# Decode attention with a gated feed-forward: outputs gathered two batches at a time, matmuls with unused results, and weight rows in another order

## The chip, the cores and the metric

The kernel runs on one NeuronCore of a Trainium2 chip, alone. The metric is the device time of one execution in microseconds (us). Each number of a run is the median over several executions; the profile is of one further execution, and its "span" is the time from its first to its last instruction.

## The reference, cut to what matters

The input has 8 rows (batches) of 512 numbers. They are normalised, and the same normalised rows go into an attention step over a cache and into a feed-forward part whose result gates the attention's output.

```python
def _A_ref(x, k_cache, v_cache, wq, wo):     # 32 query heads, 8 kv heads, Dh = 128
    W = min(4096, max(256, Sk // 4))         # Sk = 4096: the last 1024 positions
    q = (x @ wq) ...                         # one query per batch and head
    k, v = last W positions, each kv head shared by 4 query heads
    p = softmax(q k^T * Dh ** -0.5)
    return (p v) @ wo                        # wo: 4096 x 512
def _B_ref(x, w_gate, w_up, w_down):         # F = 1792
    return (gelu(x @ w_gate) * (x @ w_up)) @ w_down

xn = layernorm(x)
s = _A_ref(xn, ...)
g = silu(_B_ref(xn, ...))
return x + s * g
```

All tensors are bf16. The part of the caches that is read has 32 MB, the weights have some 14 MB, and there is one query per batch: a program of loads.

## The kernel before, in words

The order of the instructions of each engine is written out by hand (`manual_schedule`, L74); nothing is moved by a planner.

**Loads.** All large loads are issued by SyncE, in one queue. `load_wide` (L95) fills one of 3 wide buffers with 128 rows of up to 16 KB: the two halves of wq (`load_wq`, L100), w_gate and w_up (`load_up`, L113), w_down (`load_down`, L116) and the first half of wo (`load_wo`, L122). `load_kv` (L103) fills one of 14 ring buffers with 1 MB of a k or v cache; the later pieces of wo take ring buffers too. Of wq, w_gate and w_up, partition p holds the rows 4p to 4p+3 one after the other (L93, L114), so a load takes 128 contiguous rows. The loop of L494 issues the v load of group g and the k load of group g+2; in its last passes it issues w_gate, w_up, w_down (L500 to L502) and then wo in six pieces, of 16, 8, 4, 2, 1 and 1 row blocks (L505 to L510). The wide buffer of wo's first piece is w_gate's, so that load waits until w_gate's matmuls are done. The input x comes by two small loads on ScalarE's queue (L143), 8 rows each.

**Start.** x is normalised by VectorE into `xhat` (L214), turned by 4 TensorE transposes (L225) into `xT`, with the row order of the weights; then q is computed (L379), turned and laid out (L400, L408).

**Attention.** There are 16 groups, a batch and a half of the kv heads each. In pass g of the loop TensorE computes the scores of group g (`score`, L267), ScalarE their exponentials (`soft`, L293), VectorE turns them (`turn_p`, L301), and TensorE turns the k tiles of group g+1 (`turn_k`, L251) and multiplies the probabilities of group g-1 with v (`values`, L312). `gather` (L330) then takes the result of group g-1: one fp32 product with ones for the sums (L333), two with a selection matrix (L337), a reciprocal (L346) and a product on VectorE (L347) into `oT_all`.

**End.** `ffn_up` (L416) runs 16 matmuls for w_gate, regroups the attention output (L354), then 16 for w_up (all L424), and the gelu on ScalarE and VectorE. `ffn_down` (L461) runs 14 matmuls with w_down (L465), copies the result (L475), brings it into 32 rows with fp32 matmuls (L478) and forms the gate `g_sb` (L487 to L491). Last come the 128 matmuls with wo (L544), in the order of wo's pieces, most in pairs on two column groups of the array; two DVE operations after the last of them (L558, L559) and the store of 8 KB (L560).

Of the kernel before, what the change touches and what calls it, by code (L numbers as in the profile page):

```python
# [9 lines left out]
ALU = mybir.AluOpType  # L10
AX = mybir.AxisListType
BF16 = mybir.dt.bfloat16
FP32 = mybir.dt.float32
# [3 lines left out]
def kernel(  # L17
# [13 lines left out]
    nc = tc.nc  # L31

    B, Sq, D = A_x.shape
    Hkv, Sk, Dh = A_k_cache.shape[1], A_k_cache.shape[2], A_k_cache.shape[3]
# [4 lines left out]
    F = B_w_gate.shape[1]  # L39
    NDC = D // 128  # L40
# [4 lines left out]
    P = nc.NUM_PARTITIONS  # L45
# [8 lines left out]
    QW = HN * rep  # L54
# [8 lines left out]
    p_pool = ctx.enter_context(tc.tile_pool(name="p_pool", bufs=2))  # L63
    pT_pool = ctx.enter_context(tc.tile_pool(name="pT_pool", bufs=2))
    small = ctx.enter_context(tc.tile_pool(name="small", bufs=3))
    o_pool = ctx.enter_context(tc.tile_pool(name="o_pool", bufs=1))
    ffn_sb = ctx.enter_context(tc.tile_pool(name="ffn_sb", bufs=1))
    ps_t = ctx.enter_context(tc.tile_pool(name="ps_t", bufs=3, space=bass.MemoryType.PSUM))
    ps_sc = ctx.enter_context(tc.tile_pool(name="ps_sc", bufs=1, space=bass.MemoryType.PSUM))
    ps_a = ctx.enter_context(tc.tile_pool(name="ps_a", bufs=1, space=bass.MemoryType.PSUM))  # L70
# [14 lines left out]
    DQ = D // NQ  # L85
    x_sb = persist.tile([32, D], BF16, name="x_sb")
# [3 lines left out]

    wq_rows = A_wq.rearrange("(p k) n -> p (k n)", k=NDC)  # L93

    def load_wide(rows, c0, c1):  # L95
        t = wide_slot()
        nc.sync.dma_start(out=t[:, 0 : c1 - c0], in_=rows[:, c0:c1])
        return t

    def load_wq(h):  # L100
# [9 lines left out]
        )  # L110
        return t

    def load_up(w):  # L113
        return load_wide(w.rearrange("(p k) n -> p (k n)", k=NDC), 0, NDC * F)  # L114

    def load_down():  # L116
        return load_wide(B_w_down.rearrange("(p j) d -> p (j d)", j=FR), 0, FR * D)
# [25 lines left out]
    for t in range(2):  # L143
        c = slice(t * D // 2, (t + 1) * D // 2)
# [3 lines left out]
    ident = consts.tile([P, P], BF16, name="ident")  # L148
    nc.vector.memset(ident, 0.0)
    nc.gpsimd.affine_select(  # L150
        out=ident,
        in_=ident,
# [8 lines left out]
        out=perm.rearrange("p (h q) -> p h q", q=P // 32),  # L161
        in_=ident.rearrange("p (q h) -> p h q", q=P // 32),
# [3 lines left out]
    ones_f = consts.tile([P, P], FP32, name="ones_f")  # L166
# [5 lines left out]
        out=hot.rearrange("n r (m j) -> n r m j", m=HN),  # L172
# [21 lines left out]
        out=selq,  # L194
# [18 lines left out]
    nc.vector.reciprocal(out=rstd, in_=rstd)  # L213
    xhat = persist.tile([32, D], BF16, name="xhat")  # L214
    nc.vector.tensor_scalar(  # L215
        out=xhat,
        in0=x_sb,
        scalar1=mv[:, 0:1],
        scalar2=rstd[:, 0:1],
        op0=ALU.subtract,  # L220
# [3 lines left out]
    for k in range(NDC):  # L224
        nc.tensor.transpose(  # L225
            xT_ps[:, k, :],
            xhat.rearrange("b (p k) -> b k p", k=NDC)[:, k, :],
            ident[0:32, 0:32],
        )
    xT = persist.tile([P, NDC, 32], BF16, name="xT")  # L230
# [70 lines left out]
    def turn_p(g):  # L301
        p, acc = p_t[g]
        pT = pT_pool.tile([P, 512], BF16, name="pT")
        nc.vector.transpose(out=pT, in_=p)  # L304
        pT_t[g] = pT
        ss = small.tile([P, QW], FP32, name="ss")
        nc.vector.tensor_scalar(
            out=ss, in0=selq, scalar1=acc[:, 0:1], scalar2=None, op0=ALU.mult
        )
        ss_t[g] = ss  # L310

    def values(g):  # L312

# [14 lines left out]
        o_t[g] = o_sb  # L328

    def gather(g):  # L330
        b, i = groups[g]
        a_ps = ps_a.tile([P, 2, QW], FP32, name="a_ps", tag="a")
        nc.tensor.matmul(  # L333
            a_ps[:, 0, :], ones_f, ss_t[g], start=True, stop=True, skip_group_check=True
        )
        for r in range(2):
            nc.tensor.matmul(  # L337
                a_ps[:, 1, :],
                o_t[g][:, r * Dh : (r + 1) * Dh],
                selr[:, r, :],  # L340
                start=(r == 0),
                stop=(r == 1),
                skip_group_check=True,
            )
        rs = small.tile([P, QW], FP32, name="rs")
        nc.vector.reciprocal(out=rs, in_=a_ps[:, 0, :])  # L346
        nc.vector.tensor_tensor(  # L347
            out=oT_all[:, b, i * QW : (i + 1) * QW],
            in0=a_ps[:, 1, :],
            in1=rs,  # L350
            op=ALU.mult,
        )

    def regroup():  # L354

# [60 lines left out]
    def ffn_up():  # L416
        z_ps = ps_big.tile([P, 512], FP32, name="big")
        u_ps = ps_big.tile([P, 512], FP32, name="big")
        for ps, ws in ((z_ps, wg_t), (u_ps, wu_t)):
            if ps is u_ps:  # L420
                regroup()
            for k in range(NDC):
                for j in range(4):
                    nc.tensor.matmul(  # L424
                        ps[32 * j : 32 * j + 32, 0:FT],
                        xT[:, k, :],
                        ws[:, k * F + j * FT : k * F + (j + 1) * FT],
                        start=(k == 0),
                        stop=(k == NDC - 1),
                        tile_position=(0, 32 * j),  # L430
                        skip_group_check=True,
                    )
# [13 lines left out]
        nc.vector.tensor_tensor(out=u3, in0=z2, in1=zT, op=ALU.mult)  # L446
        h_sb = ffn_sb.tile([P, FT], BF16, name="h_sb")
        nc.vector.tensor_tensor(out=h_sb, in0=u3, in1=uT, op=ALU.mult)

        nc.vector.transpose(  # L450
            out=hT.rearrange("p j b -> p (j b)"),
            in_=h_sb.rearrange("b (p j) -> b j p", j=FR),
        )
# [7 lines left out]
    def ffn_down():  # L461
        f_ps = ps_big.tile([P, 512], FP32, name="big")
        for j in range(FR):
            c = j % 4
            nc.tensor.matmul(  # L465
                f_ps[32 * c : 32 * c + 32, :],
                hT[:, j, :],
                wd_t[:, j * D : (j + 1) * D],
                start=(j < 4),
                stop=(j >= FR - 4),  # L470
                tile_position=(0, 32 * c),
                skip_group_check=True,
            )
        f_sb = ffn_sb.tile([P, D], FP32, name="f_sb")
        nc.scalar.copy(out=f_sb, in_=f_ps)  # L475
        f_ps = ps_a.tile([P, DQ], FP32, name="f2_ps", tag="a")
        for q in range(NQ):
            nc.tensor.matmul(  # L478
                f_ps[0:32, :],
                push[:, NQ - 1 - q : NQ - 1 - q + 32],  # L480
                f_sb[:, q * DQ : (q + 1) * DQ],
                start=(q == 0),
                stop=(q == NQ - 1),
                skip_group_check=True,
            )
        th2 = ffn_sb.tile([32, DQ], FP32, name="th2")
        nc.scalar.activation(out=th2, in_=f_ps[0:32, :], func=ACT.Tanh, scale=0.5)  # L487
        nc.vector.tensor_scalar(
            out=th2, in0=th2, scalar1=0.5, scalar2=0.5, op0=ALU.mult, op1=ALU.add
        )  # L490
        nc.vector.tensor_tensor(out=g_sb, in0=th2, in1=f_ps[0:32, :], op=ALU.mult)  # L491


    for g in range(NGR + 1):  # L494
        if g < NGR:
            v_t[g] = load_kv(A_v_cache, *groups[g])
            if g + 2 < NGR:
                k_t[g + 2] = load_kv(A_k_cache, *groups[g + 2])
        if g == NGR - 1:
            wg_t = load_up(B_w_gate)  # L500
            wu_t = load_up(B_w_up)
            wd_t = load_down()  # L502
        if g == NGR:

            parts = [(0, 16), (16, 24), (24, 28), (28, 30), (30, 31), (31, 32)]  # L505
            wo_t = [load_wo(*q) for q in parts[:2]]
            for t in range(2):
                r = slice(16 * t, 16 * t + 16)
                nc.sync.dma_start(out=x_res[r, :], in_=x_rows[r, :])
            wo_t += [load_wo(*q) for q in parts[2:]]  # L510
        if g < NGR:
            score(g)
            soft(g)
        if g + 1 < NGR:
            turn_k(g + 1, 0)
        if g < NGR:
            turn_p(g)
        if g + 1 < NGR:
            turn_k(g + 1, 1)
        if g:  # L520
            values(g - 1)
        if g + 1 < NGR:
            turn_k(g + 1, 2)
            turn_k(g + 1, 3)
        if g:
            gather(g - 1)

    ffn_up()
    ffn_down()


# [19 lines left out]
                    skip_group_check=True,  # L551
                )
    early = ffn_sb.tile([32, DQ], FP32, name="early")
    tmp = ffn_sb.tile([32, DQ], FP32, name="tmp")
    out_sb = ffn_sb.tile([32, DQ], BF16, name="out_sb")
    nc.vector.tensor_tensor(out=early, in0=acc[1], in1=g_sb, op=ALU.mult)
    nc.vector.tensor_tensor(out=early, in0=early, in1=x_res, op=ALU.add)
# [35 lines left out]
```

## Time and profile before

| | |
|---|---|
| time, median of 11 executions (lowest to highest) | 120.92 us (120.63 to 121.92) |
| the profiled execution's own time | 121.36 us |
| its span | 119.6 us |
| bytes loaded | 47.46 MB, 397 GB/s over the span |
| DMA row in the middle of the span | 397 to 463 GB/s a slice |
| PE busy | 88.8 us (74%), 987 matmuls |
| DVE, ACT, POOL busy | 63.4, 40.6, 4.8 us |
| mean granted clock of TensorE | 0.900 |

How to read it: the page cuts the span into 40 slices of 2.99 us and prints the busy share of each engine in tenths. PEclk is the TensorE clock granted in a slice, in tenths of full speed. The chain of work that ended last is followed back from the last instruction to what released each step. The list of groups gives for a line of the kernel its count, its busy time, the mean duration of one and what it waited for. PEld is TensorE's load of the stationary operand, which overlaps the matmuls; ACT is ScalarE, DVE is VectorE, SP is SyncE.

### The profile page before, as it was taken

The page shows a single profiled execution, that of the slowest core. Times are in us where ns is not written, and L with a number is a line of the kernel's source. Part 1 is how long each engine was busy: PE and PEld are TensorE (multiplying, and loading weights), DVE is VectorE, ACT ScalarE, POOL GpSimd, SP SyncE. Part 2 cuts the span into 40 slices and gives each one's busy share as a digit, 9 for nine tenths or more (in the row PEclk, how much of TensorE's full clock was granted, in tenths as well). Part 3 has the DMA queues.
Part 4 walks back from the last instruction along what each step waited for, and adds up shares of the span by engine and source line. Part 5 has one row for each costly group of instructions (what it writes and reads, how often), then busy time and mean ns, then how long its engine had stood idle before and what let it go on. Part 6 is the DMA issues. An engine that isn't in the chain of part 4 may idle for free.

```text
span 119.6 us, 2398 instructions
## 1 busy us (share of the span) xinstructions
PE 88.8 (74%) x987; PEld 63.9 (53%) x987; DVE 63.4 (53%) x147; ACT 40.6 (34%) x78; POOL 4.8 (4%) x14
## 2 busy tenths in 40 slices
PE   0005966676999999999999797987979840466990
PEld 0005723453867777686776584665747610114990
DVE  5025644635566866876695584754947427600111
ACT  4000314692443562464346243362443302002000
POOL 5900000000000000000000000000000000000000
PEclk9999999769599999999999999999999985555589
DMA  3999999999999999999999999999999999999920
GB/s 93 428 399 463 397 427 427 430 425 419 427 433 422 427 416 430 425 433 414 427 430 430 411 430 433 430 416 425 430 430 437 436 412 446 429 447 392 392 101 3
DMA packets 6346, 47.62 MB, mean 398 GB/s; under 512 B 816, under 2 KB 1088, under 8 KB 1344
## 3 DMA queue, kind: packets, MB, share of 16 engines
q1 hardware_dynamic: 6304, 47.47, 94.5%
q8 instruction: 8, 0.13, 0.4%
q14 instruction: 2, 0.02, 0.0%
q10 hardware_dynamic: 32, 0.01, 0.0%
HBM read 47.46 MB, written 0.01 MB: 397 GB/s over the span
## 4 chain that ended last, share of the span: by engine, by line
DMA 49%; PE 30%; DVE 11%; ACT 6%; issue 2%; ACTq 0%; DVEq 0%
DMA wide_slot<-in_B_w_gate_dram 18%; DMA slot<-in_A_v_cache_dram 16%; PE t_ps L257 13%; DMA wide_slot<-in_A_wo_dram 10%; DVE kT L263 6%; PE big L544 5%; DMA x_sb<-in_A_x_dram 5%; PE sc_ps L283 4%; PE o_ps L317 3%; ACT q_all L408 2%; PE big L379 2%; DVE q_all L408 2%; ACT L296 1%; ACT L142 1%; PE big L424 1%
## 5 line engine op out<-in xcount | busy, mean ns | idle before, releaser
L263 DVE COPY kT<-t_ps 128x1024 bf16<-128x1024 bf16 x48 | 31.9, 688 | 22.1 <-PE t_ps L257 20.2
L257 PE MATMUL t_ps<-ident_f,slot 128*128 128x128 f32 x256 | 38.7, 300 | 4.0 <-DMA slot<-in_A_k_cache_dram 3.7
L257 PEld LDWEIGHTS t_ps<-ident_f,slot 128*128 128x128 f32 x256 | 30.7, 152 | 14.1 <-issue 6.8
L263 ACT COPY kT<-t_ps 128x1024 bf16<-128x1024 bf16 x16 | 16.2, 1012 | 11.8 <-PE t_ps L257 11.4
L296 ACT ACTIVATE p<-sc_ps 128x512 bf16<-128x512 f32 x16 | 9.6, 597 | 29.1 <-PE sc_ps L283 29.1
L283 PE MATMUL sc_ps<-kT,q_all 128*32 128x512 bf16 x128 | 10.1, 383 | 4.1 <-ACT q_all L408 1.8
L304 DVE STREAM_TRANSPOSE pT<-p 128x512 bf16<-128x512 bf16 x16 | 11.2, 703 | 3.3 <-ACT p L296 3.3
L317 PE MATMUL o_ps<-slot,pT 128*32 128x256 bf16 x256 | 10.3, 284 | 0.0
L337 PE MATMUL a_ps<-selr,o_sb 128*128 128x16 f32 x64 | 9.7, 264 | 0.4 <-ACT o_sb L327 0.3
L337 PEld LDWEIGHTS a_ps<-selr,o_sb 128*128 128x128 f32 x64 | 8.5, 193 | 0.6 <-ACT o_sb L327 0.6
L225 PE MATMUL t_ps<-ident,xhat 32*128 32x32 bf16 x4 | 0.3, 194 | 10.3 <-DVE xhat L215 10.3
L283 PEld LDWEIGHTS <-q_all 128*32 128x32 bf16 x128 | 3.2, 94 | 8.0 <-issue 3.2
L317 PEld LDWEIGHTS <-pT 128*32 128x32 bf16 x256 | 5.5, 98 | 2.9 <-issue 2.4
L327 ACT COPY o_sb<-o_ps 128x256 f32<-128x256 f32 x16 | 6.0, 377 | 1.3 <-PE o_ps L317 1.3
L544 PEld LDWEIGHTS <-og 128*32 128x32 bf16 x128 | 6.0, 130 | 0.7 <-DMA wide_slot<-in_A_wo_dram 0.7
L273 PE MATMUL sc_ps<-far,hot 4*128 4x512 bf16 x16 | 6.1, 384 | 0.0
L424 PE MATMUL big<-wide_slot,xT 128*32 128x448 bf16 x32 | 2.9, 500 | 4.2 <-DMA wide_slot<-in_B_w_up_dram 2.7
L225 PEld LDWEIGHTS <-xhat 32*128 32x128 bf16 x4 | 0.2, 114 | 10.3 <-DVE xhat L215 10.3
L333 PEld LDWEIGHTS a_ps<-ss,ones_f 128*128 128x128 f32 x32 | 5.1, 200 | 0.5 <-DVE oT_all L347 0.3
L333 PE MATMUL a_ps<-ss,ones_f 128*128 128x16 f32 x32 | 5.1, 234 | 0.0
L346 DVE RECIPROCAL rs<-a_ps 128x16 f32<-128x16 f32 x16 | 4.0, 249 | 1.4 <-PE a_ps L337 1.2
L408 DVE COPY q_all<-t_ps 64x128 bf16<-64x128 bf16 x4 | 2.8, 779 | 2.4 <-ACT q_all L408 1.6
(68 smaller groups left out, 55.6 us busy)
## 6 DMA issues: line engine op xcount, KB each, us to landing
slot<-in_A_k_cache_dram SPq DMA_DIRECT2D x16, 1024.0 KB, 19.5
slot<-in_A_v_cache_dram SPq DMA_DIRECT2D x16, 1024.0 KB, 19.6
wide_slot<-in_A_wq_dram SPq DMA_DIRECT2D x2, 2048.0 KB, 10.4
wide_slot<-in_A_wo_dram SPq DMA_DIRECT2D x1, 2048.0 KB, 12.1
wide_slot<-in_B_w_gate_dram SPq DMA_DIRECT2D x1, 1792.0 KB, 21.4
wide_slot<-in_B_w_up_dram SPq DMA_DIRECT2D x1, 1792.0 KB, 23.2
wide_slot<-in_B_w_down_dram SPq DMA_DIRECT2D x1, 1792.0 KB, 25.0
slot<-in_A_wo_dram SPq DMA_DIRECT2D x1, 1024.0 KB, 14.2
```

The source lines that it names most:

```text
L257: nc.tensor.transpose(kp[:, c * P : (c + 1) * P], kw[:, rp * P : (rp + 1) * P], ident_f)
L263: copy(out=kT_t[g][:, t * 8 * P : (t + 1) * 8 * P], in_=kp.bitcast(BF16))
L273: nc.tensor.matmul(sc, hot.rearrange("n r q -> n (r q)"), far, start=True, stop=False, skip_group_check=True,)
L283: nc.tensor.matmul(sc[32 * t : 32 * t + 32, :], q2_all[:, i, b, e, :, :, :].rearrange("w r n j -> w (r n j)"), kT[:, :, 32 * t : 32 * t + ...
L296: nc.scalar.activation(out=p, in_=sc_t[g], func=ACT.Exp, scale=inv_sqrt_dh, accum_out=acc)
L304: nc.vector.transpose(out=pT, in_=p)
L317: nc.tensor.matmul(o_ps[32 * u : 32 * u + 32, :], pT_t[g][:, m * 32 : (m + 1) * 32], v_t[g][:, m * 256 : (m + 1) * 256], start=(m < 4), st ...
L327: nc.scalar.copy(out=o_sb, in_=o_ps)
L333: nc.tensor.matmul(a_ps[:, 0, :], ones_f, ss_t[g], start=True, stop=True, skip_group_check=True)
L337: nc.tensor.matmul(a_ps[:, 1, :], o_t[g][:, r * Dh : (r + 1) * Dh], selr[:, r, :], start=(r == 0), stop=(r == 1), skip_group_check=True,)
L408: copy(out=q2_all[64 * rr : 64 * rr + 64, i, :, e, rr, :, :].rearrange("p b n j -> p j n b"), in_=qT_ps[64 * rr : 64 * rr + 64, :, e, :, 0 ...
L544: nc.tensor.matmul(acc[a], shifted(og, j, q), wo_t[piece][:, c0 : c0 + DQ], start=(j == rows[0] and q == 0), stop=(j == rows[-1] and q == ...
```

## The change

- **Two batches per gather.** `gather` is called in every second pass, for two groups: one product with ones for both sums, four selection products, one reciprocal and one product on VectorE for both. `ss` is a tile for two groups, and `o_pool` has two buffers.
- **Matmuls with unused results.** `keep_going(n)` runs n matmuls with a stationary operand of 32 columns and a moving one of 512 columns, into a PSUM tile that nobody reads. 12 stand between `ffn_up` and `ffn_down`, 2 within `ffn_down`, between its 14 matmuls and the fp32 matmuls that bring the result into 32 rows.
- **Rows in another order.** Of wq, w_gate and w_up, partition 8a+c now holds the rows 64c+4a to 64c+4a+3. `xhat` is written in that order, and its four transposes read contiguous columns.
- **w_gate in three loads.** The last 896 of its 7168 columns a partition come in two loads of their own, of 64 partitions each, ahead of w_up. Their source has 8 as its first dimension.
- `th2` and `tmp` share a buffer.

```diff
-    wq_rows = A_wq.rearrange("(p k) n -> p (k n)", k=NDC)
+    def blocks(w):
+        return w.rearrange("(c a k) n -> a c (k n)", c=8, k=NDC)
+    wq_rows = blocks(A_wq)
...
-    def load_up(w):
-        return load_wide(w.rearrange("(p k) n -> p (k n)", k=NDC), 0, NDC * F)
+    def load_up(w, low=0):
+        rows, n = blocks(w), NDC * F
+        t = load_wide(rows, 0, n - low)
+        if low:
+            for a in range(0, 16, 8):
+                nc.sync.dma_start(
+                    out=t[8 * a : 8 * a + 64, n - low : n], in_=rows[a : a + 8, :, n - low : n]
+                )
+        return t
...
-        out=xhat,
-        in0=x_sb,
+        out=xhat.rearrange("b (k a c) -> b c a k", a=16, c=8),
+        in0=x_sb.rearrange("b (c a k) -> b c a k", a=16, c=8),
...
     def gather(g):
-        a_ps = ps_a.tile([P, 2, QW], FP32, name="a_ps", tag="a")
+        a_ps = ps_a.tile([P, 2, 2, QW], FP32, name="a_ps", tag="a")
         nc.tensor.matmul(
-            a_ps[:, 0, :], ones_f, ss_t[g], start=True, stop=True, skip_group_check=True
-        )
-        for r in range(2):
+            a_ps[:, 0, :, :],
+            ones_f,
+            ss_t[g].rearrange("p m q -> p (m q)"),
...
+        )
+        for m in range(2):
+            for r in range(2):
+                nc.tensor.matmul(
+                    a_ps[:, 1, m, :],
+                    o_t[g + m][:, r * Dh : (r + 1) * Dh],
+                    selr[:, r, :],
...
+    def keep_going(n):
+        idle = ps_t.tile([P, 512], FP32, name="t_ps", tag="t")
+        moving = q_sb.rearrange("p i j e r w -> p (i j e r w)")
+        for _ in range(n):
             nc.tensor.matmul(
-                a_ps[:, 1, :],
-                o_t[g][:, r * Dh : (r + 1) * Dh],
-                selr[:, r, :],
+                idle[0:32, :],
+                ident[:, 0:32],
+                moving[:, 0:512],
...
+        keep_going(2)
         f_sb = ffn_sb.tile([P, D], FP32, name="f_sb")
         nc.scalar.copy(out=f_sb, in_=f_ps)
...
-            wg_t = load_up(B_w_gate)
+            wg_t = load_up(B_w_gate, 896)
             wu_t = load_up(B_w_up)
...
-        if g:
-            gather(g - 1)
+        if g and g % 2 == 0:
+            gather(g - 2)
     ffn_up()
+    keep_going(12)
     ffn_down()
```

More of the change, by code (lines that the diff above doesn't have):

```diff
@@ L65 @@
     small = ctx.enter_context(tc.tile_pool(name="small", bufs=3))
-    o_pool = ctx.enter_context(tc.tile_pool(name="o_pool", bufs=1))
+    o_pool = ctx.enter_context(tc.tile_pool(name="o_pool", bufs=2))
     ffn_sb = ctx.enter_context(tc.tile_pool(name="ffn_sb", bufs=1))
@@ L89 @@
     x_rows = x_flat.rearrange("b (q c) -> (b q) c", q=NQ)
-    wq_rows = A_wq.rearrange("(p k) n -> p (k n)", k=NDC)
+    def blocks(w):
+        return w.rearrange("(c a k) n -> a c (k n)", c=8, k=NDC)
+    wq_rows = blocks(A_wq)
     def load_wide(rows, c0, c1):
         t = wide_slot()
-        nc.sync.dma_start(out=t[:, 0 : c1 - c0], in_=rows[:, c0:c1])
+        nc.sync.dma_start(out=t[:, 0 : c1 - c0], in_=rows[..., c0:c1])
         return t
@@ L226 @@
             xT_ps[:, k, :],
-            xhat.rearrange("b (p k) -> b k p", k=NDC)[:, k, :],
+            xhat[:, k * P : (k + 1) * P],
             ident[0:32, 0:32],
@@ L305, in turn_p @@
         pT_t[g] = pT
-        ss = small.tile([P, QW], FP32, name="ss")
+        if g % 2 == 0:
+            ss_t[g] = small.tile([P, 2, QW], FP32, name="ss")
         nc.vector.tensor_scalar(
-            out=ss, in0=selq, scalar1=acc[:, 0:1], scalar2=None, op0=ALU.mult
+            out=ss_t[g - g % 2][:, g % 2, :], in0=selq, scalar1=acc[:, 0:1], scalar2=None, op0=ALU.mult
         )
-        ss_t[g] = ss
     def values(g):
@@ L331, in gather @@
         b, i = groups[g]
-        a_ps = ps_a.tile([P, 2, QW], FP32, name="a_ps", tag="a")
+        a_ps = ps_a.tile([P, 2, 2, QW], FP32, name="a_ps", tag="a")
         nc.tensor.matmul(
-            a_ps[:, 0, :], ones_f, ss_t[g], start=True, stop=True, skip_group_check=True
-        )
-        for r in range(2):
-            nc.tensor.matmul(
-                a_ps[:, 1, :],
-                o_t[g][:, r * Dh : (r + 1) * Dh],
-                selr[:, r, :],
-                start=(r == 0),
-                stop=(r == 1),
-                skip_group_check=True,
-            )
-        rs = small.tile([P, QW], FP32, name="rs")
-        nc.vector.reciprocal(out=rs, in_=a_ps[:, 0, :])
+            a_ps[:, 0, :, :],
+            ones_f,
+            ss_t[g].rearrange("p m q -> p (m q)"),
+            start=True,
+            stop=True,
+            skip_group_check=True,
+        )
+        for m in range(2):
[4 more added lines that the diff above has]
+                    selr[:, r, :],
+                    start=(r == 0),
+                    stop=(r == 1),
+                    skip_group_check=True,
+                )
+        rs = small.tile([P, 2, QW], FP32, name="rs")
+        nc.vector.reciprocal(out=rs, in_=a_ps[:, 0, :, :])
         nc.vector.tensor_tensor(
-            out=oT_all[:, b, i * QW : (i + 1) * QW],
-            in0=a_ps[:, 1, :],
+            out=oT_all[:, b : b + 2, i * QW : (i + 1) * QW],
+            in0=a_ps[:, 1, :, :],
             in1=rs,
@@ L352, in gather @@
         )
+    def keep_going(n):
+        idle = ps_t.tile([P, 512], FP32, name="t_ps", tag="t")
+        moving = q_sb.rearrange("p i j e r w -> p (i j e r w)")
+        for _ in range(n):
+            nc.tensor.matmul(
+                idle[0:32, :],
+                ident[:, 0:32],
+                moving[:, 0:512],
+                start=True,
+                stop=True,
+                skip_group_check=True,
+            )
     def regroup():
@@ L485, in ffn_down @@
             )
-        th2 = ffn_sb.tile([32, DQ], FP32, name="th2")
+        th2 = ffn_sb.tile([32, DQ], FP32, name="th2", tag="th")
         nc.scalar.activation(out=th2, in_=f_ps[0:32, :], func=ACT.Tanh, scale=0.5)
@@ L553 @@
     early = ffn_sb.tile([32, DQ], FP32, name="early")
-    tmp = ffn_sb.tile([32, DQ], FP32, name="tmp")
+    tmp = ffn_sb.tile([32, DQ], FP32, name="tmp", tag="th")
     out_sb = ffn_sb.tile([32, DQ], BF16, name="out_sb")
```

## The prediction

> **What bounds the kernel now.** I read the page first, part 2 above all. In its 40 slices of 2.99 us the DMA row is full from the second slice to the 38th, and two other rows say what happens behind it:
>
> ```profile
> PE   0005966676999999999999797987979840466990
> ...
> PEclk9999999769599999999999999999999985555589
> DMA  3999999999999999999999999999999999999920
> ```
>
> The loads keep all 16 DMA engines busy until about 115.3 us, so nothing that PE or DVE saves before that shortens the loads. What can be saved lies behind the last load, or in how evenly the 16 engines finish. The PEclk row drops to half speed for the stretch of the feed-forward part and of the last matmuls. The chain of work that ended last, its final pieces, says what the end consists of:
>
> ```profile
> 98.44 12.06 DMA wide_slot<-in_A_wo_dram
> 110.50 0.04 issue
> 110.54 6.22 PE big L544 x128
> 116.76 0.02 issue
> 116.78 0.29 DVE tmp L558
> ```
>
> From 110.54 on nothing waits for a transfer: L544 runs its 128 matmuls in 6.22 us without a gap, then two DVE operations and the store of the output. The query of L544's own instructions adds that the durations change on the way:
>
> ```profile
> L544 PE MATMUL big<-wide_slot,og x64: 287/314/314, 110.5 to 113.8; 128*32 128x128 bf16 x64
> L544 PE MATMUL big<-slot,og x64: 219/219/314, 113.9 to 116.5; 128*32 128x128 bf16 x64
> ```
>
> In the records of the single instructions, the 128 matmuls start in 72 steps: 56 pairs and 16 singles. Steps are 106.7 ns apart until 114.8 us and 55.8 ns apart afterwards. Windows of 3.41 us, laid on the places where the clock changed, show what went before (columns: length, PE busy, PEld, DVE, ACT, POOL, granted clock, DMA share, GB/s):
>
> ```profile
> 26.05:29.46 3.41, 1.74 (x17) 0.98 (x16) 2.11 (x5) 1.48 (x3) 0.00 (x0) 1.00 1.01 420
> 94.31:97.73 3.42, 1.76 (x26) 1.26 (x22) 1.04 (x4) 0.37 (x1) 0.00 (x0) 1.00 1.01 432
> 15.80:19.22 3.42, 2.21 (x36) 1.20 (x28) 1.68 (x3) 1.17 (x2) 0.00 (x0) 1.00 1.01 429
> 107.97:111.38 3.41, 2.73 (x26) 2.08 (x28) 0.49 (x2) 0.58 (x2) 0.00 (x0) 0.50 0.96 402
> 111.38:114.79 3.41, 3.41 (x70) 3.41 (x68) 0.00 (x0) 0.00 (x0) 0.00 (x0) 0.50 0.84 323
> 22.63:26.05 3.42, 3.21 (x16) 2.45 (x13) 1.14 (x3) 2.80 (x5) 0.00 (x0) 0.50 1.02 431
> ```
>
> After a window with 51% of PE busy the clock fell, after 65% it stayed; at half clock, 80% did not lift it, 94% and 100% did.
>
> [...] the x_sb loads, of 8 rows, left packets on eight engines only; call these the first eight. [...] The trace has eight such packets on queue 8, spaced like PE's work, and each of the seven that fell among the loads held its DMA engine up by about 1.41 us.
>
> **The engines' finish.** Following the packet records engine by engine: when w_down ends, the engines without a fetch are done by 103.6 to 104.6 us, six with one by 105.1 to 105.3. Four of these six are among the first eight (fetches at 41.9, 67.1, 77.4, 92.1 us). A seventh, of the other eight, is delayed at 111.9. So the last load of wo ends on seven engines at 115.06 to 115.26, of the first eight at most 115.16, on the others at 113.5 to 114.6. A landing reaches PE 0.36 to 0.43 us after the last packet (w_gate 96.79 to 97.15, w_down 105.31 to 105.74); I use 0.39.
>
> **The change, part by part.**
>
> *Gathering in pairs.* Per pair, L333 goes from 4 instructions to 2 and L337 stays at 8: 16 matmuls of about 0.26 us less on PE, 8 reciprocals (0.25) and 8 products (0.18) less on DVE. All of it lies under the loads: worth nothing. The last gather does two batches at once, 0.6 us (four matmuls of L337) later at the end of attention. It is covered by the 1.52 us for which PE waits for w_gate; with that cover gone it would cost 0.6.
>
> *xhat in another order.* The one operation (0.40 us) writes with a stride, which this trace doesn't show: between 0 and 0.6 us more (up to two and a half times as long). PE starts its transposes later by that; the loads do not wait for it, and PE makes it up in the 3.7 us that it waits for k loads later. Zero.
>
> *Other rows of wq, w_gate, w_up.* The same bytes in packets of the same size. The first packets of wq took 1.0 to 1.4 us instead of 0.61; with other addresses this start could be up to 0.3 us shorter or longer. I take zero and keep both ends.
>
> *w_gate in three loads.* Two issues more, 0.33 us each, ahead of w_up and w_down on SP's queue; SP issued these 23 and 25 us before they landed, so it is covered; without cover, 0.7. The main load shrinks from 14336 to 12544 B a row. Packet pitches are 607 ns (16384 B), 532 (14336), 306 (8192), 80 (2048), 42 (1024), which gives 466 for 12544 and 71 for 1792: every engine saves 8 x 66 = 0.53 us. The two small loads have 8 as their slowest dimension, so all 128 rows go to the first eight engines: 16 x 71 plus two semaphore packets = 1.15 us. Net: +0.62 us on the first eight, -0.53 on the other eight. Where the fetches fall is not shown for the new program; I assume the same engines. Then the end of all loads moves from 115.26 to 115.16 + 0.62 = 115.78, and lands at 116.17.
>
> *The 12 matmuls.* 512 columns take 4 x 106.7 = 0.43 us at half clock, 0.22 at full. w_up lands at about 102.05, its matmuls take 1.68 (the same as now), and the twelve follow without a wait: up to 5.1 us more, 6.8 in one piece, which always contains a whole window. So the clock is full between 105.1 and 108.9, and the twelve end between 107.0 and 108.9. Queued behind them is w_down's product, L465, which could have started at 106.25 (w_down's landing, 0.6 later than now): a delay of 0.8 to 2.6 us. It then runs at full clock, 1.0 instead of 1.89.
>
> *The 2 matmuls* run beside the copy of f_sb (0.59 us): 0.43, zero, or 0.26 if the clock is at half. L478 takes about 1.0 instead of 1.89. L544 is free to start at 109.8 to 111.7.
>
> *The end.* wo's first piece lands at about 111.05, so L544 starts at 111.05 to 111.7. 72 steps of 55.8 ns are 4.02 us: PE alone would be done by 115.9. Now the transfers end last: the last piece lands at 116.17, its 4 steps and one matmul's length are 0.39, giving 116.56 where it is 116.75 now. The tail behind it (2.88 us) is unchanged. **Sum:** the profiled execution had a span of 119.6 within 121.36 us; the new span is 119.4. That is -0.2, and from the median of 120.92, which lies 0.44 below the profiled execution, 120.7. Own range 120.2 to 121.1.
>
> **The rivals.**
>
> *The delays fall on the other eight engines* (0.25). For it: the shift, 0.62 + 0.53, nearly fills the 1.41 us of a fetch. Against: four fetches sat on the first eight. Then the loads end at 115.26 - 0.53 = 114.73, the last piece lands at 115.12, PE is through at 115.5: 1.2 us less, 119.7.
>
> *The clock falls back* (0.17). With landings setting the pace, PE idles between pieces. From w_down on I count 68 to 79% busy a window, above the 65% that kept the clock, but L478's matmuls counted for little at 107.97. If the last 24 steps run at 106.7 ns from wo2's landing at 114.83, PE ends at 117.6: +0.85, 121.8.
>
> *The twelve do not lift the clock* (0.13). They fill 32 of 128 columns, and no row shows such a stream alone. Slower if at 111 us the clock is still half: w_down's product starts at 108.85, takes 1.89, the two matmuls 0.85, L478 1.89, so L544 starts at 113.5 and runs cold for 3.4 to 6.8 us before it lifts the clock itself: PE ends at 119.2 to 120.1, +2.5 to +3.3. About 123.9.
>
> **How the numbers follow.** The measurement tells 0.3%, 0.36 us. The forecast (0.45) is faster by more than that in about a third of its own range, when the start of the loads gains or a fetch falls better: 0.16 faster, 0.25 same, 0.04 slower. The first rival is faster (0.25). Falling back is slower for 0.11 and the same for 0.06; the last is slower (0.13). Faster 0.41, same 0.31, slower 0.28. The range runs from 119.6 to 122.0, which leaves out the last rival and little else.
>
> **What would show it.** L544's steps at 55.8 ns from its first, PEclk 9 from about slice 36: the twelve worked. PE waiting for wo pieces inside L544, the last wait ending near 116.2: the loads are the bound. A last landing near 115.1 is the first rival. L465 starting at 107 to 109 shows the price of the twelve. Wrong if L544 is still cold at 112, if L544 starts after 112, or if the main loads lose their 425 to 430 GB/s.

## The result and the profile after

The changed kernel takes 141.27 us (median of 12 executions, 140.15 to 143.12) against 120.92 us for the kernel before (47 executions): ratio 1.166, 95% interval 1.163 to 1.169. The ratios of this document leave out executions over 1.5% longer than the fastest of their kernel, so they are not exactly those of the medians. The changed kernel is 20 us slower. The prediction was 120.7 us, at most 122.0, so it missed altogether. The profiled execution has a span of 139.7 us where it was 119.6.

Part 2 of the page of the changed kernel says where to look. A slice is now 3.49 us long:

```profile
DMA  4899999999999999999999999999999999899940
GB/s 131 192 232 289 288 225 197 413 434 422 425 427 422 434 425 417 429 425 427 420 432 427 415 436 420 429 427 417 412 187 222 209 214 218 271 434 422 407 154 2
```

The DMA row is as full as before. The GB/s row is not: in slices 2 to 7, and again in slices 30 to 35, equally busy engines move 187 to 289 GB/s instead of some 425. The first stretch is that of wq (with the first caches between its halves), the second that of w_gate and w_up. A full DMA row is no proof that the loads run well; here it hides a loss of 20 us.

The same stretches in windows, first of the changed kernel, then of the kernel before (start and end, length, then busy time and count of PE, PEld, DVE, ACT and POOL, granted clock, DMA share, GB/s):

```profile
1.50:24.00 22.50, 5.72 (x36) 4.06 (x37) 6.73 (x15) 2.10 (x4) 4.46 (x10) 1.00 0.98 237
24.00:99.00 75.00, 64.56 (x684) 44.48 (x683) 46.28 (x90) 33.61 (x65) 0.00 (x0) 0.91 1.01 424
99.00:120.00 21.00, 9.25 (x90) 6.25 (x87) 6.77 (x16) 3.31 (x8) 0.00 (x0) 0.62 1.04 232
120.00:134.50 14.50, 11.42 (x148) 6.35 (x148) 2.10 (x4) 0.85 (x2) 0.00 (x0) 0.73 0.93 383
```

```profile
1.50:17.50 16.00, 6.58 (x52) 4.39 (x52) 6.32 (x17) 2.13 (x5) 4.46 (x10) 1.00 0.98 401
17.50:90.90 73.40, 64.75 (x697) 47.51 (x697) 47.69 (x105) 34.47 (x66) 0.00 (x0) 0.95 1.01 426
90.90:101.10 10.20, 5.83 (x74) 3.68 (x74) 4.87 (x15) 2.44 (x6) 0.00 (x0) 0.83 1.02 432
101.10:115.30 14.20, 10.22 (x138) 7.02 (x139) 3.02 (x6) 0.85 (x2) 0.00 (x0) 0.52 0.93 387
```

The attention in the middle runs at 424 GB/s where it had 426, the last loads at 383 where they had 387. Only the loads whose rows were reordered lost their rate: 237 for 401 at the start, 232 for 432 in the feed-forward part.

The packet records say it load by load. A 16384-byte packet of wq takes 1.23 us in the median instead of 0.61, a 14336-byte packet of w_up 1.07 instead of 0.535, a 12544-byte packet of w_gate 0.91. The medians of k and v (8192 bytes, 0.309), wo (0.61) and w_down (0.54) are unchanged. The packet times summed and divided by 16 engines grew by 8.3 us for the 16384-byte packets (15.2 to 23.5), by 10.2 for w_gate, w_up and w_down with the two small loads (12.9 to 23.1), and by 1.2 for k and v, which run beside the slow loads: 19.7 of the 20.1 us by which the span grew. The other 0.4 lie behind the store, whose last packet ends 1.58 us before the end of the span where it was 1.19.

In the chain of waits, a load of wq now stands at the start with 22.9 us; before, wq was no piece of the chain. w_gate's piece has grown from 21.4 to 23.8 us, and the end follows a late piece of wo, with 32 of the last 128 matmuls:

```profile
2.16 22.91 DMA wide_slot<-in_A_wq_dram
...
89.94 23.83 DMA wide_slot<-in_B_w_gate_dram
...
116.19 18.56 DMA slot<-in_A_wo_dram
```

PE's longest waits between 95 and 136 us are for the two loads (waiting engine and line, what it waited for, total, times, longest). L458 was L424, and the kernel before follows:

```profile
PE big L458 <- DMA wide_slot<-in_B_w_up_dram: 7.5, 1, 7.5
PE big L458 <- DMA wide_slot<-in_B_w_gate_dram: 3.5, 1, 3.5
```

```profile
PE big L424 <- DMA wide_slot<-in_B_w_up_dram: 2.7, 1, 2.7
...
PE big L424 <- DMA wide_slot<-in_B_w_gate_dram: 1.5, 1, 1.5
```

So the cause is in how fast the reordered loads run, and the experiments ask why.

### The profile page after: what moved, and what is told of

Read it like the earlier page. It is cut to its first block, busy times and chain, and to the rows that moved or that the text cites. A ratio compares the mean times of both kernels' runs of the same rounds, so it can differ in the third digit from the quotient of the medians.

```text
span 139.7 us, 2381 instructions
## 1 busy us (share of the span) xinstructions
PE 92.7 (66%) x985; PEld 62.5 (45%) x985; DVE 63.3 (45%) x131; ACT 40.6 (29%) x78; POOL 4.8 (3%) x14
## 4 chain that ended last, share of the span: by engine, by line
DMA 61%; PE 25%; DVE 7%; ACT 2%; SPq 2%; issue 1%; DVEq 0%
DMA wide_slot<-in_B_w_gate_dram 17%; DMA wide_slot<-in_A_wq_dram 16%; DMA slot<-in_A_v_cache_dram 14%; DMA slot<-in_A_wo_dram 13%; PE t_ps L270 12%; DVE kT L276 5%; PE sc_ps L296 4%; PE o_ps L330 3%; PE a_ps L357 2%; PE big L580 1%; DVE q_all L442 1%; ACT q_all L442 1%; PE big L413 1%; PE t_ps L434 1%; PE sc_ps L286 1%
## 5 line engine op out<-in xcount | busy, mean ns | idle before, releaser
L270 PEld LDWEIGHTS t_ps<-ident_f,slot 128*128 128x128 f32 x256 | 31.5, 155 | 11.0 <-issue 8.3
L330 PE MATMUL o_ps<-slot,pT 128*32 128x256 bf16 x256 | 10.8, 292 | 2.8 <-DMA slot<-in_A_v_cache_dram 2.8
L458 PE MATMUL big<-wide_slot,xT 128*32 128x448 bf16 x32 | 3.9, 570 | 11.1 <-DMA wide_slot<-in_B_w_up_dram 7.5
L357 PE MATMUL a_ps<-selr,o_sb 128*128 128x16 f32 x64 | 9.2, 277 | 0.0
L296 PEld LDWEIGHTS <-q_all 128*32 128x32 bf16 x128 | 2.0, 94 | 12.1 <-DVE kT L276 8.4
L458 PEld LDWEIGHTS <-xT 128*32 128x32 bf16 x32 | 1.3, 124 | 12.9 <-issue 12.0
L413 PE MATMUL big<-wide_slot,xT 128*32 128x512 bf16 x32 | 3.5, 588 | 3.2 <-DMA wide_slot<-in_A_wq_dram 3.2
L366 DVE RECIPROCAL rs<-a_ps 128x32 f32<-128x32 f32 x8 | 2.9, 358 | 6.2 <-PE a_ps L357 6.2
L379 PE MATMUL t_ps<-q_sb,ident 128*32 128x512 bf16 x14 | 5.4, 553 | 0.0
L222 DVE BATCH_NORM_STATS2 stats<-x_sb 32x6 f32<-32x512 bf16 x1 | 0.7, 682 | 10.0 <-DMA x_sb<-in_A_x_dram 10.0
## 6 DMA issues: line engine op xcount, KB each, us to landing
slot<-in_A_v_cache_dram SPq DMA_DIRECT2D x16, 1024.0 KB, 20.1
```

The lines of the kernel that those rows point to most:

```text
L270: nc.tensor.transpose(kp[:, c * P : (c + 1) * P], kw[:, rp * P : (rp + 1) * P], ident_f)
L296: nc.tensor.matmul(sc[32 * t : 32 * t + 32, :], q2_all[:, i, b, e, :, :, :].rearrange("w r n j -> w (r n j)"), kT[:, :, 32 * t : 32 * t + ...
L330: nc.tensor.matmul(o_ps[32 * u : 32 * u + 32, :], pT_t[g][:, m * 32 : (m + 1) * 32], v_t[g][:, m * 256 : (m + 1) * 256], start=(m < 4), st ...
L357: nc.tensor.matmul(a_ps[:, 1, m, :], o_t[g + m][:, r * Dh : (r + 1) * Dh], selr[:, r, :], start=(r == 0), stop=(r == 1), skip_group_check= ...
L379: nc.tensor.matmul(idle[0:32, :], ident[:, 0:32], moving[:, 0:512], start=True, stop=True, skip_group_check=True,)
L413: nc.tensor.matmul(q_ps[i][32 * j : 32 * j + 32, :], xT[:, k, :], wq_t[k // 2][:, k % 2 * Hq * Dh + n0 : k % 2 * Hq * Dh + n0 + 512], star ...
```

## The experiments

Three explanations were open. The first and leading one: a load whose source has 16 as its first dimension is split into groups of 8 neighbouring partitions, and this grouping at the destination slows it; by what mechanism was a guess of mine that no run shows. The second: rows read from far apart in HBM are slow. The third: short loads of few rows, or a source pattern with one more dimension, are slow as such.

### The tail alone, and the order alone

**tail_only** is the changed kernel with the old row order and w_gate in one load; the gathers in pairs and the 14 matmuls stay.

```diff
     def blocks(w):
-        return w.rearrange("(c a k) n -> a c (k n)", c=8, k=NDC)
+        return w.rearrange("(p k) n -> p (k n)", k=NDC)
...
-        out=xhat.rearrange("b (k a c) -> b c a k", a=16, c=8),
-        in0=x_sb.rearrange("b (c a k) -> b c a k", a=16, c=8),
+        out=xhat,
+        in0=x_sb,
...
-            wg_t = load_up(B_w_gate, 896)
+            wg_t = load_up(B_w_gate)
```

> The change with the old row order and with w_gate in one load: only the gathering in pairs, the 12 and the 2 matmuls are left. If the loss lies in the loads of the reordered weights (my theory), this one has none of it: the 14336-byte and 16384-byte packets take 0.54 and 0.61 us again, the loads end near 115.3 us, and the last wo piece sets the end: span 118.9, about 120.2 us, 0.7 below the kernel before. If the 12 matmuls or the paired gather cost a good part of the 20 us (rival), it stays above 125.

Measured: 120.79 us (14 executions) against 120.89 (19), ratio 0.9995, interval 0.998 to 1.001. The rate is back (packets of 0.535 and 0.61 us), so nothing of the 20 us is in the gathers or the 14 matmuls. Span of the profiled execution: 119.0. The time is 0.6 us above the 120.2 that I expected; the account of the prediction comes back to that.

**rows_only** is the kernel before with the new order of wq, w_gate and w_up (`blocks` with c=8, and `xhat` written in that order), and nothing else.

> The kernel before with wq, w_gate and w_up in the new row order, each in one load, nothing else changed. If the order alone slows the loads (theory), about 20 us come back: 139 to 142 us, with 225 to 290 GB/s while these three weights are loaded. If the two small loads on eight engines hold the queue up (rival), this stays within 3 us of the kernel before.

Measured: ratio 1.152, interval 1.146 to 1.158, that is some 18.4 us. The profiled execution was the longest of the four, with a span of 140.7 us where the others have 136.6 to 138.3. Its page shows the same two valleys:

```profile
GB/s 130 186 206 267 331 210 182 375 419 436 424 426 422 426 431 410 433 419 431 417 438 415 436 417 436 415 436 419 415 191 216 212 232 208 285 430 417 403 133 2
```

w_gate and w_up both have 14336-byte packets here, at 1.07 us in the median, and run at 218 GB/s (101 to 121 us). The order of the rows alone accounts for nearly the whole loss.

### Which side: source rows or destination partitions

**near_far** and **near_far2** take the kernel before and split w_gate, w_up and w_down into eight loads of 16 rows each. Source rows and destination partitions are either neighbours ("near") or 8 apart ("far"), independently, so partitions get other rows than the reference's.

```diff
+    def load_16(rows, near_src, near_dst):
+        t = wide_slot()
+        for j in range(8):
+            src = slice(16 * j, 16 * j + 16) if near_src else slice(j, 128, 8)
+            dst = slice(16 * j, 16 * j + 16) if near_dst else slice(j, 128, 8)
+            nc.sync.dma_start(out=t[dst, 0 : NDC * F], in_=rows[src, 0 : NDC * F])
+        return t
```

near_far has w_gate from near to far, w_up far to far, w_down far to near:

> The kernel before, with w_gate, w_up and w_down each in 8 loads of 16 rows, so that each of the 16 engines gets one row of 14336 bytes a load. The 16 source rows of a load are neighbours in memory (near) or 8 apart (far), and so are the 16 partitions that they go to. w_gate: source near, partitions far. w_up: both far. w_down: source far, partitions near. The mixed two put rows in partitions where they don't belong, so the feed-forward's numbers are not the reference's. If near source addresses are the cause, w_gate alone is slow (1.0 us a packet and some 220 GB/s, against 0.54 and 425). If near partitions are the cause, w_down alone is slow. If the two-level source pattern is the cause, none is slow.

near_far2 has w_gate near to near, w_up near to far, w_down far to far:

> As the run of 16-row loads before it, with the cases dealt out otherwise: w_gate both near, w_up source near and partitions far, w_down both far (w_up's rows are in partitions where they don't belong, so the feed-forward's numbers are not the reference's). Near sources as the cause: w_gate and w_up slow, w_down fast. Near partitions as the cause: w_gate alone slow. Two-level pattern as the cause: none slow.

Measured, one execution each: 137.95 and 137.28 us. All six loads are slow. Windows inside w_gate, w_up and w_down, near_far first, then near_far2:

```profile
91.00:98.50 7.50, 4.29 (x57) 3.07 (x56) 3.20 (x11) 1.32 (x4) 0.00 (x0) 0.89 1.05 243
99.00:106.00 7.00, 2.01 (x17) 0.63 (x17) 1.40 (x3) 0.54 (x1) 0.00 (x0) 0.50 1.05 250
107.00:116.00 9.00, 1.69 (x16) 0.54 (x16) 2.43 (x4) 0.00 (x0) 0.00 (x0) 0.50 0.99 172
```

```profile
91.00:101.00 10.00, 5.30 (x57) 3.82 (x56) 3.17 (x11) 1.32 (x4) 0.00 (x0) 0.69 1.08 184
102.50:109.50 7.00, 2.01 (x17) 0.63 (x17) 1.33 (x3) 0.54 (x1) 0.00 (x0) 0.50 1.00 231
110.00:116.00 6.00, 1.68 (x16) 0.53 (x16) 1.95 (x4) 0.35 (x1) 0.00 (x0) 0.50 1.05 261
```

The loads with far partitions move 231 to 261 GB/s, those with near partitions 172 and 184. Source rows matter little: in these windows the median packet takes 1.03 and 1.04 us from near to far, 1.00 and 1.02 from far to far, 1.37 from near to near and 1.28 from far to near. So it is the destination that decides, and far source rows are not the slower ones, which speaks against the second explanation. But I had not expected far partitions to be slow at all, and the third explanation was still alive, since every load here was short.

In rates: the plain loads of 128 rows moved 426 to 432 GB/s in the kernel before, far partitions 231 to 261, near ones 172 and 184. Why the partitions matter is not shown: the packet records name neither the engine of a packet nor the partition that it fills.

### Groups of four in place of groups of eight

**rows4** is the whole change with groups of 4 partitions, 32 as the first dimension of the source; w_gate's last 896 columns come in four loads of 32 partitions. The rows of one group are still far apart in HBM. It asks whether groups of eight partitions are what costs the rate.

```diff
-        return w.rearrange("(c a k) n -> a c (k n)", c=8, k=NDC)
+        return w.rearrange("(c a k) n -> a c (k n)", c=4, k=NDC)
...
-            for a in range(0, 16, 8):
+            for a in range(0, 32, 8):
                 nc.sync.dma_start(
-                    out=t[8 * a : 8 * a + 64, n - low : n], in_=rows[a : a + 8, :, n - low : n]
+                    out=t[4 * a : 4 * a + 32, n - low : n], in_=rows[a : a + 8, :, n - low : n]
```

> The whole change with 4 in place of 8 in the row order: partition 4a+c holds the rows 128c+4a on, the source has 32 as its first dimension, and the last 896 columns of w_gate come in four loads of 32 partitions, still with 8 as their first dimension. [...] Then the packets take 0.54 and 0.61 us again and the time is 120.0 to 121.2 us. Rivals: any source order with rows far apart, or a two-level source pattern, is slow. Then it stays at 135 us or more.

**rows4_whole** is the same with w_gate in one load, `load_up(B_w_gate)`.

> As the run before it, with w_gate in one load. Tells what the shift of w_gate's last columns to eight engines is worth once the order is harmless: if the delays of the instruction blocks fall mostly on the other eight, the run with the shift is 0.3 to 0.6 us faster than this one; if they fall on both, it is 0 to 0.6 slower. [...] 120.3 to 121.0 us. Rivals: 135 us or more.

Measured: rows4 123.34 us, ratio 1.018 (1.016 to 1.021); rows4_whole 121.14 us, ratio 1.0025 (1.001 to 1.004). The GB/s row of rows4_whole:

```profile
GB/s 88 352 423 459 434 399 423 421 437 432 407 432 432 432 407 429 434 418 426 423 432 423 426 423 423 434 410 440 423 429 425 428 457 428 423 431 415 405 189 3
```

rows4_whole has no valley; its packets take 0.535 and 0.61 us as in the kernel before. Far-apart source rows and a source pattern with an extra dimension cost the loads no rate once the groups are of four. That takes the second explanation out, and the pattern's shape with it. The 0.25% left, 0.3 us, fit the start: SyncE takes 0.65 us to issue the first load of wq with the extra dimension instead of 0.40, and its first packet starts at 2.23 us instead of 1.84.

The difference between the two, 2.2 us, is the price of the separate loads. I had expected at most 0.6 either way, and rows4 itself at 121.2 at most. Slices 32 and 33 of rows4's page (378 and 340 GB/s) show the place. The window before it and the place itself:

```profile
91.00:95.00 4.00, 2.90 (x46) 2.08 (x48) 2.51 (x6) 0.99 (x4) 0.00 (x0) 0.95 1.03 434
95.00:99.20 4.20, 4.20 (x40) 2.88 (x33) 1.00 (x3) 0.37 (x1) 0.00 (x0) 0.50 1.03 329
```

While eight engines carry the small packets (74 ns each; rows4 has 848 packets under 512 bytes where rows4_whole has 816, eight more for each of the four loads) and the others are already at w_up, w_up's packets take 0.78 us in the median. 4.2 us at 329 instead of 434 GB/s (rows4_whole's figure for that window) is by estimate 1.0 us lost for all engines. The small packets are some 1.2 us more for these eight, less the 0.5 that the shorter main load saves. Together that fits the 1.7 us by which the last load ends later: its last packet ends at 117.25 us in rows4, at 115.56 in rows4_whole.

The spans differ by 2.4 us (121.6 and 119.2), and the other 0.7 have nothing to do with the rate of the loads. The store's last packet ends 1.93 us before the end of rows4 and 1.20 before that of rows4_whole. SyncE checks the semaphores of the transfers one after another at the end; in rows4 four such checks come after the one for the store, in rows4_whole none. The other two traces show the same: none after it in the kernel before, four in the changed kernel, at 138.55 to 138.78 us.

### Short loads as such

**eight** takes the kernel before with w_gate, w_up and w_down in sixteen loads of 8 rows each. All three are equally short and differ in the partitions of a load, and in its source rows, which go along with them: 4 apart within 32 partitions, 8 apart within 64, and neighbours.

```diff
...
+    step4 = [slice(32 * m + j, 32 * m + 32, 4) for m in range(4) for j in range(4)]
+    step8 = [slice(64 * m + j, 64 * m + 64, 8) for m in range(2) for j in range(8)]
+    step1 = [slice(8 * m, 8 * m + 8) for m in range(16)]
...
```

> The kernel before, with w_gate, w_up and w_down each in 16 loads of 8 rows, one row of 14336 bytes for each of eight engines. The partitions of a load are 4 apart in w_gate [...], 8 apart in w_up [...], neighbours in w_down [...]. [...] a packet takes 0.54 us in w_gate, about 1.1 in w_up and near 2 in w_down, where successive loads don't overlap. If small loads as such are slow, or the source, all three are alike.

Measured: 145.76 us, one execution. Windows inside the three loads:

```profile
92.00:100.00 8.00, 3.36 (x52) 2.42 (x44) 2.24 (x8) 1.32 (x4) 0.00 (x0) 0.80 0.48 185
104.00:116.00 12.00, 0.46 (x5) 0.10 (x1) 2.58 (x5) 1.12 (x2) 0.00 (x0) 0.50 0.51 118
117.00:126.00 9.00, 1.69 (x16) 0.54 (x16) 1.60 (x2) 0.00 (x0) 0.00 (x0) 0.50 0.49 163
```

The DMA share is about one half, 0.48 to 0.51: eight rows keep eight engines busy. Among these eight, the median packet takes 0.535 us at 4 apart and 1.00 at 8 apart. So a short load is not slow as such; with near_far, where source rows made little difference, this points to the partitions. The third load missed what I expected of it: its packets took 0.81 us up to 121 us and 0.59 after that, not about 2. That 2 was an estimate of mine that no run had shown, and no run tells why it was too high.

### The same addresses, only the grouping changed

**same_rows** reads w_gate and w_up in the old order, but through a pattern of two levels: w_gate as 16 groups of 8 rows, w_up as 32 groups of 4. Each group starts 256 bytes further back than the old order has it, once more with every group (3.8 and 7.9 KB for the last ones), so that the levels are not merged into one; the feed-forward part thus computes with shifted weights.

```diff
...
+    def load_split(w, first):
+        row = NDC * F
+        inner = P // first
+        src = bass.AP(
+            tensor=w.tensor,
+            offset=w.offset,
+            ap=[[inner * row - 128, first], [row, inner], [1, row]],
+        )
+        return load_wide(src, 0, row)
...
-            wg_t = load_up(B_w_gate)
-            wu_t = load_up(B_w_up)
+            wg_t = load_split(B_w_gate, 16)
+            wu_t = load_split(B_w_up, 32)
```

> The kernel before with its old row order, every weight in one load; only the shape of two source patterns is changed. w_gate is read as 16 groups of 8 rows, w_up as 32 groups of 4, and to keep the groups from being merged into 128 rows each group starts 256 bytes earlier than it should, so that w_gate's and w_up's values are shifted and the feed-forward's numbers are not the reference's. wq and w_down are left alone. If the first dimension of 16 is the cause [...], w_gate's packets take about 1.05 us and w_up's 0.54, from nearly the same addresses as in the kernel before: some 4 us more in all, about 125. If the far-apart source rows of the new order were the cause after all, both take 0.54 us and the time is 121.

Measured: 125.91 us, one execution, with 120.76 for the kernel before on the same chip. Here are the window of w_gate, one of the change-over, and one of w_up after w_gate's last packets, then PE's wait for w_gate:

```profile
90.90:99.00 8.10, 4.29 (x57) 3.16 (x57) 3.20 (x11) 1.32 (x4) 0.00 (x0) 0.87 1.03 240
99.00:103.50 4.50, 1.11 (x16) 0.49 (x15) 0.00 (x0) 0.00 (x0) 0.00 (x0) 0.50 0.99 303
102.00:105.30 3.30, 2.01 (x17) 0.70 (x17) 0.86 (x2) 0.54 (x1) 0.00 (x0) 0.50 1.01 430
```

```profile
PE big L434 <- DMA wide_slot<-in_B_w_gate_dram: 6.0, 1, 6.0
```

w_gate's packets take 1.05 us, w_up's 0.535 in the median. Until about 102 us, when the last of w_gate's end, w_up's packets take some 1.0 us as well: a slow load also holds up the one beside it. In rows4_whole, where no load is slow, groups of four run at 0.535 us from the first packet. Both weights read nearly the addresses of the kernel before, into the same partitions. With a first dimension of 16 the load runs at 240 GB/s, with 32, once alone, at 430. This is the shortest form of the cause; why 16 is slow no run shows. PE's wait for w_gate goes from 1.5 to 6.0 us, 4.5 of the 5.1 us by which this kernel is longer.

### The kernel before, profiled once more

**before_again** is the kernel before, unchanged.

> The kernel before, unchanged, for a second profile. The first profiled execution had a span of 119.6 us and took 121.36, which is 0.44 above the median. If the 0.7 us that the tail alone was to gain vanished because a usual execution of the kernel before already ends earlier (its last matmuls get the full clock sooner), this one has a span near 119.0 and L544 changes from 106.7 to 55.8 ns steps before 114.8 us. If it again ends at 116.7 us on PE, the gain went elsewhere.

Measured: 121.22 us with a span of 119.5. Its last 128 matmuls are again cold (granted clock 0.50) until 114.47 us, as in the first profile, and end at 116.6. The executions of the kernel before that ran next to tail_only had spans from 118.9 to 119.5, with 119.0 in the middle. So a profiled execution with 119.5 or 119.6 sits at the upper end, and the typical one is 0.5 us better.

## Why the prediction was wrong, step by step

**The step that failed: other rows of wq, w_gate and w_up.** I wrote "The same bytes in packets of the same size" and took zero, with 0.3 us either way for the start. Measured alone (rows_only) it is some +18.4 us. Bytes and packet sizes are indeed the same; what changed is the source's first dimension, 16 where it was 128, and a packet took 1.07 us where I had priced it at 0.53 (1.23 for 0.61 in wq). Why the grouping costs that is not shown; near_far points to the destination partitions. I had asked how many engines share a load, and only for the loads with 8 as first dimension. For the 16 the answer is still sixteen (DMA share 1.04 in the window from 99 to 120 us); what had to be asked as well was into groups of how many partitions the load is split. I had also named the sign that would prove me wrong, main loads losing their 425 to 430 GB/s, without giving it a chance or a price. None of my three rivals was about the rate of the main loads, so the range could not hold the time.

**w_gate in three loads: the shift was right, the rest left out.** I priced a small packet at 71 ns from one start to the next; in rows4 its record is 74 ns long, 3 more as with the other sizes (535 for 532), but in the changed kernel 140. What I left out is that the small loads also slow the packets of w_up beside them (0.78 us for 0.535), by estimate 1.0 us, and that the end behind the store can grow, here by 0.7: with the shift of 0.6 this makes up the 2.2 us between rows4 and rows4_whole. All this is with four small loads; with two it was not measured apart.

**The twelve matmuls: right.** In tail_only, from the twelve to the end (windows as above):

```profile
103.30:106.70 3.40, 3.40 (x13) 1.17 (x8) 1.61 (x2) 0.00 (x0) 0.00 (x0) 0.50 0.99 424
106.70:110.10 3.40, 3.06 (x29) 1.58 (x26) 0.00 (x0) 0.59 (x1) 0.00 (x0) 1.00 0.97 412
110.10:113.50 3.40, 2.42 (x76) 2.10 (x76) 0.49 (x2) 0.27 (x1) 0.00 (x0) 1.00 1.01 405
113.50:116.90 3.40, 2.48 (x62) 2.06 (x56) 1.12 (x4) 0.00 (x0) 0.00 (x0) 1.00 0.29 101
```

After one full window (PE busy for 3.40 of 3.40 us) the clock is at 1.00 from 106.7 us, within the 105.1 to 108.9 that I gave. w_down's product starts at 106.8; I had the twelve end between 107.0 and 108.9. The clock doesn't fall back although PE then fills 71 to 90% of a window. For this execution that refutes two rivals, the falling back and the twelve not lifting. My window of 3.41 us rests on the kernel before, where the granted clock is 0.50 for stretches of 3.41, 3.41 and 17.07 us (five times 3.41), from 22.63, 29.46 and 97.73 us on.

The last matmuls are at full clock from the first one, as the group of L580 in tail_only shows:

```profile
L580 PE MATMUL big<-wide_slot,og x64: 219/219/230, 110.8 to 112.5; 128*32 128x128 bf16 x64
L580 PE MATMUL big<-slot,og x64: 216/219/229, 113.2 to 115.9; 128*32 128x128 bf16 x64
```

PE now waits for pieces of wo and ends 0.78 us after the last load's end (115.36 to 116.14), which is my 0.39 for the landing and 0.39 for the last steps. In the changed kernel the same happens 20 us later: the granted clock is 1.00 in the window from 127.9 to 136.4 us, and L513's eight matmuls take 1.03 us where L478's took 1.89.

**The end: right for the profiled execution, wrong for the median.** tail_only has the old loads, so its end follows from 115.26 us for the last packet, giving a span of 118.9 by my own sum; it has 119.0. But this is no gain against the median. I had subtracted a saving from a profiled execution that was 0.44 us above the median and then carried the saving over to the median in full. The executions of tail_only have spans from 118.8 to 119.3, those of the kernel before from 118.8 to 119.8 over two comparisons (one of 46 has 120.9). The middle one is at 118.9 for tail_only, at 119.0 and 119.1 for the kernel before. Most executions of the kernel before therefore already end near the limit of the loads. What the twelve matmuls seem to do is cut off the late ones. Only the ratio of 0.9995 is shown; that the typical execution before lifts its clock earlier is argued from its span, since no profile of one was taken. Their mean granted clock (0.885 to 0.911, with 0.900 and 0.886 in the two profiled ones) doesn't settle it, as a window at half clock counts the same early or late.

**The gathers in pairs: right.** In tail_only PE still waits 1.4 us for w_gate (1.5 before), so the later last gather stays covered, as I had it.

**xhat in another order: too small, and hidden as said.** The row of the operation before and after (shortest, median and longest ns, its start):

```profile
L215 DVE TENSOR_SCALAR xhat<-x_sb,mv,rstd x1: 401/401/401, 9.8 to 9.8; 32x512 bf16<-32x512 bf16 x1
```

```profile
L228 DVE TENSOR_SCALAR xhat<-x_sb,mv,rstd x1: 1581/1581/1581, 14.5 to 14.5; 32x512 bf16<-32x512 bf16 x1
```

It costs 1.18 us where my bound was 0.6. It ends at 16.1 us, and PE waits for wq's second half until 25.1, so no time is lost by it here.

**Instruction fetches: my assumption is not confirmed.** I took the eight packets of 16384 bytes on queue 8, the page's "q8 instruction", for the fetches, and assumed that they fall on the same engines in the new program. Followed from packet to packet, those of tail_only at 27.1, 42.3, 54.6 and 67.2 us seem to fall on engines of the second eight. But the records don't name the engines, and the paths cross, so which eight a fetch falls on is uncertain, in the prediction too; so is whether the small loads use the eight engines of the x_sb loads. The 1.41 us by which a fetch holds its engine up come out of the records of the kernel before at each of six fetches: 0.89 to 0.96 us for the fetch, and 0.45 to 0.55 more than usual for the packet behind it.

## What to carry to other kernels

Before a load's pattern is changed, ask two things of its first dimension: how many engines share it, and into groups of how many partitions it splits the load. Here sixteen groups of eight partitions nearly halved the rate (218 to 240 GB/s for some 430) and thirty-two groups of four, or a plain load of 128 rows, kept it; the DMA row stayed full in both cases, so read the GB/s row or the time of one packet. Why the partitions matter is not shown here; the rates are. And set a saving against the spread of the executions: where the profiled one is above the median, part of what it shows as waste is not there in the usual run.

## What the runs showed that I had not expected

- A load of 16 groups of 8 neighbouring partitions moved 218 to 240 GB/s where the plain one moved 430; packets of 14336 bytes went from 0.535 to 1.05 us or more, in one run with nearly the same addresses in HBM and the same partitions in all (same_rows).
- Loads of 16 rows were slow however their partitions were laid: 231 to 261 GB/s at 8 apart, 172 to 184 as neighbours.
- Four small loads of 56 KB on eight engines made the last load end 1.7 us later in a kernel bound by its loads, by estimate 1.0 of it through slower packets of the large load beside them. Another 0.7 us were lost behind the store.
- The strided write of one 32x512 tile in bf16 took 1.58 us instead of 0.40.
